# The last tile of a gated-recurrence and GEGLU kernel: its output in one piece or in two halves of the columns

## The chip, the cores and the metric

The kernel runs on one core of one Trainium2 chip. The metric is device time in microseconds (us) from launch to end, as a median over several runs. 0.3% of it is 0.78 us.

## What is computed

The first part is a complex gated recurrence over 768 steps for 4 batches and 8 heads of width 48. The second part takes its result, 3072 tokens of width 384, through a gated feed-forward block with a gated residual:

```python
S_re, S_im = a * S + k v^T                 # per step, a = a_re + i a_im, capped at 0.999
y[t] = q[t] @ S_re                         # -> x, 3072 x 384
ffn_out = gelu(x @ w_gate) * (x @ w_val) @ w_out      # d_ff = 1536
res_gate = 1 / (1 + exp(-(x @ w_res)))
out = x + res_gate * ffn_out               # float32
```

## The kernel before

The sequence is cut into chunks of 128 tokens, so there are 24 tiles of 128 tokens by 384 columns (4 batches, 6 chunks). The tiles are handled in units of one or two: units 0 and 1 are single first chunks, units 2 to 11 hold two tiles each, and the last pair is split into units 12 and 13 with one tile each. Three functions work on a unit `p`: `prepare` (loads, logarithms, running sums, features), `attend` (scores, state and x) and `forward` (the feed-forward block).

Nothing is run when these functions are called. Each call of `add` records a step: its engine, a kind, a function that issues the instructions, and the values that it reads and writes. `plan.run` then issues all 1450 steps in the order of a list, `ORDER`, written out by hand, and picks the buffers by it. The layer beneath derives the semaphore waits from the instructions in that order. `PLACE` moves some steps to another engine than their default, by step number. A second rule is in `run`: the kinds named in `PORT` (line 26; "otx", the sum with x, is one of them, while "ot", the gate product, is not) are chained, so that such a step on VectorE waits for the last such step on GpSimd, and the other way round.

The steps of `forward` that matter here, with the lines of the profile:

- L592: the products x @ w_gate and x @ w_val into PSUM banks ("gv"); L597: gelu on ScalarE; L598: its product with the value half on VectorE ("h").
- L607: x @ w_res ("res"); L609: the tanh that becomes the gate, `sg`, on ScalarE.
- L618: the output product, 12 matrix products of 384 columns into one PSUM bank, issued as three steps of four ("out").
- L622: the gate product on VectorE, (sg + 1) times the bank, into the SBUF tile `ot` ("ot").
- L625: the sum with x, in place in `ot` ("otx"), on GpSimd or, by `PLACE`, on VectorE. The last two tiles have it on VectorE.
- L627: the store of `ot`, 128 rows of 1536 bytes, from SyncE's queue ("store"). All 24 stores go out there; ScalarE issues no DMA in this kernel.

`ORDER` ends with unit 12. The tail of the list, in words: unit 13's output product, gate product and sum; unit 12's x @ w_res; unit 12's last four output products; its tanh; unit 13's store; unit 12's gate product, sum and store. At the end of the program (L665) SyncE waits for all DMA lanes and engines in a fixed row of waits, and all engines meet in barriers.

Of the kernel before, what the change touches and what calls it, by code (L numbers as in the profile page):

```python
# [15 lines left out]
OP = mybir.AluOpType  # L16
# [11 lines left out]


PLACE = {  # L30
    33: "DVE", 50: "DVE", 64: "ACT", 105: "DVE", 114: "DVE", 116: "POOL", 121: "DVE", 131: "DVE", 134: "ACT", 190: "DVE",
    191: "DVE", 213: "DVE", 221: "ACT", 223: "DVE", 225: "ACT", 230: "ACT", 245: "DVE", 305: "DVE", 306: "DVE", 323: "POOL",
    330: "DVE", 340: "DVE", 342: "ACT", 353: "DVE", 435: "ACT", 438: "ACT", 456: "DVE", 460: "DVE", 469: "DVE", 539: "DVE",
    551: "ACT", 554: "POOL", 555: "POOL", 562: "DVE", 570: "ACT", 572: "DVE", 576: "DVE", 599: "DVE", 654: "DVE", 667: "ACT",
    671: "POOL", 678: "DVE", 688: "DVE", 690: "ACT", 692: "DVE", 695: "ACT", 771: "DVE", 783: "ACT", 787: "POOL", 804: "DVE",
    806: "ACT", 811: "ACT", 817: "DVE", 831: "DVE", 872: "DVE", 899: "DVE", 902: "POOL", 903: "POOL", 943: "DVE", 1014: "POOL",
    1015: "POOL", 1022: "DVE", 1033: "ACT", 1041: "DVE", 1088: "DVE", 1124: "POOL", 1125: "POOL", 1143: "ACT", 1204: "DVE",
    1298: "DVE", 1314: "DVE", 1324: "ACT", 1325: "POOL", 1376: "DVE", 1386: "DVE", 1396: "ACT", 1397: "POOL", 1401: "DVE",
    1448: "DVE",
}  # L40
ORDER = [
    294, 293, 97, 16, 98, 303, 17, 102, 295, 21, 180, 103, 22, 104, 296, 304, 105, 23, 179, 106, 24, 107, 178, 25, 108, 109,
# [24 lines left out]
    1012, 902, 1208, 493, 503, 667, 385, 285, 592, 650, 379, 505, 903, 691, 591, 778, 96, 584, 1000, 381, 391, 692, 651, 687,  # L67
    1217, 473, 593, 907, 780, 404, 762, 393, 1013, 1311, 763, 487, 681, 585, 794, 596, 405, 890, 286, 781, 683, 594, 1312, 406,
    551, 777, 597, 1218, 600, 685, 595, 407, 908, 904, 688, 689, 905, 601, 398, 1110, 906, 408, 578, 686, 694, 399, 690, 764,
    782, 797, 698, 990, 507, 695, 579, 909, 291, 1378, 400, 699, 708, 706, 795, 1313, 766, 696, 709, 586, 618, 911, 509, 693,  # L70
    614, 292, 707, 796, 1014, 494, 489, 1105, 1122, 710, 587, 602, 697, 711, 589, 409, 512, 401, 880, 1123, 622, 1314, 799, 610,
    624, 878, 628, 620, 1001, 879, 495, 496, 891, 612, 606, 991, 513, 603, 1111, 910, 881, 623, 497, 629, 700, 616, 798, 615,
    608, 717, 599, 604, 801, 800, 895, 701, 712, 1219, 716, 514, 588, 805, 625, 1124, 515, 882, 802, 1125, 892, 897, 713, 803,
    896, 617, 1214, 619, 894, 605, 883, 783, 1220, 516, 1015, 804, 520, 893, 517, 806, 807, 621, 812, 521, 1383, 1379, 914, 808,
    1126, 598, 522, 1384, 1002, 814, 702, 523, 809, 822, 824, 815, 718, 524, 813, 912, 1019, 823, 734, 525, 518, 703, 626, 993,
    825, 1129, 607, 627, 916, 736, 738, 609, 1020, 920, 826, 720, 913, 726, 1130, 827, 918, 744, 1003, 1127, 816, 728, 611,
    1021, 740, 519, 915, 636, 1004, 1007, 613, 919, 705, 1016, 817, 1315, 1221, 1017, 630, 992, 1006, 704, 637, 1008, 833, 1018,
    1009, 1385, 631, 1005, 1128, 638, 1131, 832, 1010, 1022, 719, 936, 898, 1386, 727, 1024, 1222, 917, 934, 639, 921, 1230,
    937, 632, 1132, 1382, 402, 721, 723, 1215, 633, 1023, 735, 1231, 935, 1210, 1322, 846, 634, 737, 1394, 924, 1211, 1133, 729,
    739, 1011, 715, 925, 842, 1134, 1101, 741, 926, 640, 818, 730, 927, 995, 1323, 722, 819, 899, 714, 742, 1395, 1212, 724,  # L80
    1112, 850, 745, 725, 928, 403, 852, 1223, 828, 938, 848, 752, 1100, 1026, 929, 732, 834, 1113, 743, 641, 731, 836, 1025,
    838, 939, 944, 847, 1028, 840, 858, 844, 945, 733, 835, 859, 829, 746, 837, 1030, 810, 860, 1027, 811, 1117, 1032, 1114,
    849, 1227, 1232, 1115, 753, 1118, 1233, 1031, 1119, 1224, 1229, 747, 820, 1228, 1316, 1309, 839, 1387, 831, 1029, 1116, 748,
    841, 1226, 922, 1225, 1234, 1135, 1324, 994, 940, 855, 1235, 1388, 1103, 1396, 854, 923, 830, 749, 1045, 1325, 754, 635,
    941, 966, 856, 755, 1397, 1104, 861, 930, 1236, 1047, 1237, 857, 1120, 950, 1213, 1238, 1048, 750, 968, 1038, 1036, 1046,
    946, 1033, 751, 1137, 843, 1308, 948, 1039, 1049, 821, 851, 1102, 1239, 1050, 952, 1037, 958, 1139, 1240, 845, 868, 1317,
    960, 1398, 853, 1055, 1040, 931, 1326, 942, 951, 1041, 1241, 869, 1244, 1054, 1399, 1042, 1034, 962, 1318, 1136, 862, 964,
    870, 943, 1327, 953, 863, 1121, 1035, 1138, 959, 1051, 1328, 1319, 1242, 1142, 756, 871, 864, 1043, 1251, 1060, 865, 1380,
    1068, 1400, 1141, 1320, 961, 970, 1321, 1056, 872, 1140, 1246, 972, 1064, 1243, 1058, 1381, 1057, 971, 1401, 973, 873, 1076,
    1389, 1066, 1044, 1072, 1143, 1245, 954, 1329, 1052, 1249, 1074, 1080, 1059, 956, 947, 1333, 1062, 1146, 1250, 932, 1155,  # L90
    1081, 963, 1147, 1078, 1144, 1390, 1157, 757, 967, 1145, 1158, 1247, 1148, 949, 1391, 955, 965, 1392, 1310, 1393, 1065,
    1149, 1061, 1248, 957, 969, 980, 1403, 1332, 1150, 1330, 1063, 1077, 1402, 1156, 1073, 1331, 1079, 981, 1151, 1404, 1164,
    1159, 1334, 974, 1406, 1070, 1258, 1075, 982, 866, 1160, 1067, 1260, 1165, 1152, 933, 1082, 1261, 975, 983, 1336, 1252,
    1083, 976, 1253, 1084, 1053, 867, 1161, 1259, 984, 1069, 977, 1186, 1071, 1182, 1188, 1153, 1262, 1335, 1184, 1085, 1337,
    1338, 1263, 1170, 978, 1192, 1265, 1405, 1254, 1183, 1407, 1090, 1255, 1408, 1175, 1185, 1086, 1154, 1409, 1091, 1087, 1256,
    1088, 1171, 1257, 1162, 1089, 1166, 1264, 1174, 1168, 1187, 979, 1176, 1092, 985, 1172, 1189, 1193, 1178, 1177, 1167, 1093,
    1180, 1173, 1190, 1094, 1413, 1191, 1266, 1271, 1411, 1270, 1341, 1272, 1274, 1342, 1179, 1276, 1169, 1292, 1268, 1273,
    1287, 1414, 1275, 1163, 1278, 1410, 1277, 1267, 1181, 1286, 1412, 1194, 1269, 1288, 1415, 1280, 1289, 1195, 1293, 1416,
    1200, 1417, 1339, 1279, 1340, 1283, 1282, 1196, 1284, 1290, 1285, 1343, 1281, 1201, 1344, 1197, 1294, 1345, 1291, 1198,
    1300, 1438, 1199, 1295, 1095, 1430, 1301, 1431, 1302, 1202, 1303, 1296, 1304, 1203, 1358, 1362, 1419, 1364, 1204, 1350,  # L100
    1440, 1297, 1205, 1354, 1360, 1298, 1427, 1432, 1418, 1356, 1299, 1422, 1420, 1305, 1434, 1421, 1435, 1436, 1351, 1352,
    1423, 1424, 1353, 1355, 1433, 1426, 1359, 1428, 1346, 1429, 1347, 1348, 1425, 1439, 1361, 1363, 1441, 1367, 1349, 1444,
    1437, 1357, 1442, 1365, 1366, 1445, 1368, 1443, 1369, 1372, 1446, 1373, 1447, 1370, 1448, 1374, 1371, 1449, 1375, 1376,
    1377,
]


# [19 lines left out]
class Plan:  # L127
# [10 lines left out]
    def add(self, eng, kind, fn, reads=(), writes=(), size=1, act=None):  # L138
        deps = set()
        for v in reads:  # L140
            deps.update(v.writers)
        for v in writes:
            deps.update(v.writers)
            deps.update(v.readers)
        stores = [v.store for v in list(reads) + list(writes) if v.store is not None]
        stores = sorted(set(stores), key=stores.index)
        t = Step(eng, kind, fn, deps, stores, size, act)
        t.index = len(self.steps)
        for v in writes:
            v.writers, v.readers = [t], []  # L150
        for v in reads:
            if t not in v.writers:
                v.readers.append(t)
        for x in stores:
            x.users.append(t)
        self.steps.append(t)
        return t
# [30 lines left out]
def kernel(  # L188
# [13 lines left out]
    nc = tc.nc  # L202
# [3 lines left out]
    DM = H * D  # L206
    FF = moe_w_gate.shape[1]
    KF = DM // 128
    NF = FF // 128
# [6 lines left out]
    NU = len(units)  # L216
    where = {bc: (p, i) for p, u in enumerate(units) for i, bc in enumerate(u)}
    size = [len(u) for u in units]

    ctx.enter_context(tc.manual_schedule())  # L220
    cst = ctx.enter_context(tc.tile_pool(name="cst", bufs=1))
# [26 lines left out]
    wo = cst.tile([128, NF, DM], BF, name="wo")  # L248
# [76 lines left out]
    on = {"DVE": nc.vector, "POOL": nc.gpsimd, "ACT": nc.scalar}  # L325
    add = plan.add

    def place(default):

        return PLACE.get(len(plan.steps), default)  # L330
# [6 lines left out]
    W = {}  # L337
# [226 lines left out]
    def forward(p):  # L564
        s, n = st[p], size[p]
        s["xT"], s["h2"] = Buf("xT"), Buf("h2")
        xT = [s["xT"].part() for _ in range(n)]
        for i in range(n):
            if p >= PE_X:
                add("SP", "dX", lambda i=i: nc.sync.dma_start(  # L570
                    out=s["xT"].tile[:, :, i, :], in_=s["x"].tile[:, i].rearrange("p h d -> p (h d)"), transpose=True), [s["xi"][i]], [xT[i]])
# [3 lines left out]
            def f(i=i, xp=xp):  # L575
                xp.make([128, KF, 128], BF)
                for k_ in range(KF):
                    nc.tensor.transpose(out=xp.tile[:, k_, :],
                                        in_=s["x"].tile[:, i].rearrange("p h d -> p (h d)")[:, k_ * 128:(k_ + 1) * 128], identity=ident)
# [3 lines left out]
        h2 = []  # L583
        for m in range(NF // 2):
            gp, vp, hh = Bank(), Bank(), s["h2"].part()
            h2.append(hh)
            for name, w_, o_ in (("wg", wg, gp), ("wv", wv, vp)):
# [11 lines left out]
                out=hv(), in0=hv(), scalar=0.5, in1=vp.tile, op0=OP.mult, op1=OP.mult), [vp], [hh], n)  # L599
        sg = [Buf("sg") for _ in range(n)]  # L600
# [9 lines left out]
                [rp], [sg[i]], 1, "G")  # L610
        for i, (b, c) in enumerate(units[p]):
            op_, ot = Bank(), Buf("ot")
            for lo in range(0, NF, 4):
                def f(i=i, lo=lo, op_=op_):
                    if lo == 0:
                        op_.make([128, DM])
                    for k_ in range(lo, lo + 4):
                        nc.tensor.matmul(out=op_.tile, lhsT=s["h2"].tile[:, k_, i * 128:(i + 1) * 128], rhs=wo[:, k_, :],  # L618
                                         start=(k_ == 0), stop=(k_ == NF - 1))
                add("PE", "out", f, [h2[lo // 2], h2[lo // 2 + 1], W["wo", lo]], [op_])  # L620
            ti = b * NC + c
            add("DVE", "ot", lambda i=i, op_=op_, ot=ot: nc.vector.scalar_tensor_tensor(  # L622
                out=ot.tile, in0=sg[i].tile, scalar=1.0, in1=op_.tile, op0=OP.add, op1=OP.mult), [sg[i], op_], [ot])
            e8 = place("POOL")
            add(e8, "otx", lambda i=i, ot=ot, e8=e8: on[e8].tensor_tensor(  # L625
                out=ot.tile, in0=ot.tile, in1=s["x"].tile[:, i].rearrange("p h d -> p (h d)"), op=OP.add), [s["xi"][i]], [ot])
            add("SP", "store", lambda ot=ot, ti=ti: nc.sync.dma_start(out=out[ti * 128:(ti + 1) * 128, :], in_=ot.tile), [ot], [])  # L627

    weights()
    for p in range(NU):  # L630
# [39 lines left out]
```

## Time and profile before

| what | value |
|---|---|
| median of 3 runs (lowest to highest) | 260.29 us (260.19 to 260.85) |
| the profiled execution | 261.98 us, of which the span 260.2 us |
| mean granted TensorE clock | 0.974, lower in slices 6 to 8 of 40 and full after them |
| busy share of the span: TensorE, VectorE, ScalarE, GpSimd | 85%, 87%, 81%, 35% |
| store, issue to landing, 24 of them: min / median / max | 1.9 / 2.5 / 4.3 us |
| last matrix product ends, last sum ends, last store issued | 255.8, 257.1, 257.1 us |

How to read it: times of instructions are counted from the start of the span. The 1.8 us between the span and the execution's time lie outside what the profile shows. The engine rows say how long an engine was busy, not that it set the end; what sets the end is read from the chain of work that ended last and from the timeline of the last microseconds. "SPq" is SyncE's queue of DMA issues and waits.

### The profile page before, as it was taken

The numbers are of one execution on the slowest core, as the hardware profiler recorded it, in microseconds if no ns is written. First come the engines' busy times: TensorE is split into PE (matmuls) and PEld (weight loads), VectorE is DVE, ScalarE is ACT, GpSimd is POOL, SyncE is SP. The second block draws the span as 40 slices with busy tenths as digits, with TensorE's granted clock in tenths as the row PEclk, the third lists the DMA queues.
The fourth block names the chain that finished last, engine by engine and source line by source line (L and its number), as shares of the span: only waits on it lengthen the run. The fifth ranks groups of instructions, "written<-read, shape, count | busy, mean of one in ns | idle before, by whom it ended". The sixth has DMA issues, their size and how long they took to land.

```text
span 260.2 us, 6343 instructions
## 1 busy us (share of the span) xinstructions
PE 222.3 (85%) x2415; PEld 174.7 (67%) x2415; DVE 225.7 (87%) x401; ACT 211.3 (81%) x354; POOL 90.4 (35%) x116
## 2 busy tenths in 40 slices
PE   0233842877999999999999999999999999999993
PEld 0011532757878877887887778768778778877881
DVE  2789999997999999999999999999999976573463
ACT  4899999998999999999999999797999932532330
POOL 1022266594611662486626177006020230101100
PEclk9999975799999999999999999999999999999999
DMA  8999999999999998999986779779789539201311
GB/s 140 188 186 186 188 185 167 205 181 217 152 183 185 164 199 161 192 178 183 214 147 121 153 155 168 181 145 232 131 134 222 97 88 170 75 3 35 113 40 60
DMA packets 162174, 39.83 MB, mean 153 GB/s; under 512 B 155616, under 2 KB 162144, under 8 KB 162144
## 3 DMA queue, kind: packets, MB, share of 16 engines
q1 hardware_dynamic: 157696, 35.53, 78.1%
q0 software_dynamic: 4448, 3.90, 9.7%
q8 instruction: 19, 0.31, 0.6%
q14 instruction: 11, 0.09, 0.1%
HBM read 31.26 MB, written 4.72 MB: 138 GB/s over the span
## 4 chain that ended last, share of the span: by engine, by line
PE 60%; DVE 19%; DMA 7%; SPq 5%; issue 4%; POOL 1%; ACT 0%; DVEq 0%; POOLq 0%; ACTq 0%
PE pb L592 30%; PE pb L618 16%; SPq L374 5%; PE pb L607 3%; PE pb L360 3%; PE pb L522 3%; DMA t<-fr 2%; PE pb L492 2%; DVE h L598 2%; DMA k<-in_k_dram 2%; DMA ai<-in_a_im_dram 2%; DVE fQ L475 2%; DVE Qe L470 2%; DVE ll L408 1%; DMA vf<-in_v_dram 1%
## 5 line engine op out<-in xcount | busy, mean ns | idle before, releaser
L597 ACT ACTIVATE h<-pb 128x512 bf16<-128x512 f32 (+1 forms) x84 | 41.1, 550 | 23.5 <-PE pb L592 23.1
L592 PE MATMUL pb<-xT,wg 128*128 128x256 bf16 (+1 forms) x504 | 56.0, 257 | 1.2 <-DVE U L552 0.9
L592 PE MATMUL pb<-xT,wv 128*128 128x256 bf16 (+1 forms) x504 | 57.0, 257 | 0.0
L618 PE MATMUL pb<-wo,h 128*128 128x384 bf16 x288 | 55.5, 326 | 0.0
L598 DVE SCALAR_TENSOR_TENSOR h<-h,pb 128x512 bf16<-128x512 bf16 (+1 forms) x84 | 48.0, 601 | 7.3 <-ACT h L597 4.6
L592 PEld LDWEIGHTS <-wg 128*128 128x128 bf16 x504 | 43.1, 98 | 8.1 <-issue 1.6
L592 PEld LDWEIGHTS <-wv 128*128 128x128 bf16 x504 | 42.2, 98 | 6.1
L639 ACT ACT_TABLE_LOAD x34 | 43.6, 1283 | 1.3 <-PEq L654 0.7
L525 DVE TENSOR_TENSOR am<-pb,mask 128x512 bf16<-128x512 f32 x48 | 31.6, 680 | 4.5 <-PE pb L522 4.3
L618 PEld LDWEIGHTS <-h 128*128 128x128 bf16 x288 | 26.0, 97 | 13.8 <-issue 0.3
L625 POOL TENSOR_TENSOR ot<-ot,x 128x384 f32<-128x384 f32 x18 | 16.9, 941 | 46.1 <-issue 19.9
L444 POOL TENSOR_TENSOR tl<-t,th 128x768 fp32r<-128x768 f32 (+1 forms) x9 | 13.2, 1479 | 22.7 <-DVE Gb L554 14.3
L522 PE MATMUL pb<-QT,KT 96*128 96x128 bf16 x192 | 16.7, 219 | 2.7 <-DVE KT L335 2.4
L622 DVE SCALAR_TENSOR_TENSOR ot<-sg,pb 128x384 f32<-128x384 f32 x24 | 13.1, 547 | 6.3 <-PE pb L618 6.2
L360 PE MATMUL pb<-lh,ut_hf 128*128 128x384 f16 x24 | 8.6, 360 | 11.1 <-DVE lh L406 11.1
L398 POOL TENSOR_TENSOR t<-t,ai 128x768 f32<-128x768 f32 (+1 forms) x9 | 14.7, 1637 | 8.8 <-DMA ai<-in_a_im_dram 3.5
L522 PEld LDWEIGHTS <-KT 96*128 96x128 bf16 x192 | 12.7, 97 | 6.5 <-DVE KT L335 2.9
L492 PE MATMUL pb<-ident,fK 128*128 128x128 bf16 x112 | 10.7, 252 | 6.8 <-DVE fK L475 6.0
L609 ACT ACTIVATE sg<-pb 128x384 f32<-128x384 f32 x24 | 11.9, 499 | 5.2 <-PE pb L607 3.2
L607 PE MATMUL pb<-wr,xT 128*128 128x384 bf16 x72 | 15.6, 326 | 0.3 <-DVE am L525 0.2
L334 ACT CAST x<-pb 128x384 bf16<-128x384 f32 x19 | 9.2, 482 | 6.4 <-PE pb L536 6.1
L360 PE MATMUL pb<-th,ut_hf 128*128 128x384 f16 x24 | 8.6, 359 | 6.4 <-DVE th L335 6.0
(89 smaller groups left out, 467.3 us busy)
## 6 DMA issues: line engine op xcount, KB each, us to landing
ar<-in_a_re_dram SPq DMA_DIRECT2D x24, 192.0 KB, 4.6
ai<-in_a_im_dram SPq DMA_DIRECT2D x24, 192.0 KB, 4.7
q<-in_q_dram SPq DMA_DIRECT2D x24, 192.0 KB, 4.6
k<-in_k_dram SPq DMA_DIRECT2D x24, 192.0 KB, 4.1
vf<-in_v_dram SPq DMA_DIRECT2D x24, 192.0 KB, 4.0
out_dram<-ot SPq DMA_DIRECT2D x24, 192.0 KB, 2.5
wg<-in_moe_w_gate_dram POOLq DMA_DIRECT2D x6, 192.0 KB, 7.1
wv<-in_moe_w_val_dram POOLq DMA_DIRECT2D x6, 192.0 KB, 6.2
```

The source lines that it names most:

```text
L360: nc.tensor.matmul(out=bank.tile, lhsT=ones, rhs=x[:, i * DM:(i + 1) * DM], start=(j == 0), stop=(j == 1))
L398: add(e1, "tai", lambda: on[e1].tensor_tensor(out=F("t"), in0=F("t"), in1=flat(T("ai"), n), op=OP.mult), [s["ai"]], [s["t"]], n)
L492: nc.tensor.transpose(out=tp.tile[:, h, :], in_=s[g].tile[:, i * H + h], identity=ident)
L522: nc.tensor.matmul(out=ap.tile[:, h, :], lhsT=kT.tile[0:DD, u * H // 2 + h, :], rhs=qT.tile[0:DD, u * H // 2 + h, :], start=True, stop=True)
L525: add("DVE", "am", lambda u=u, am=am, ap=ap: nc.vector.tensor_tensor(out=am.tile[:, u * H // 2:(u + 1) * H // 2, :], in0=ap.tile, in1=mask ...
L592: nc.tensor.matmul(out=o_.tile[:, u, :], lhsT=w_[:, k_, (2 * m + u) * 128:(2 * m + u + 1) * 128], rhs=s["xT"].tile[:, k_, 0:n].rearrange(" ...
L597: add("ACT", "gelu", lambda gp=gp, hv=hv: nc.scalar.activation(out=hv(), in_=gp.tile, func=AF.Gelu), [gp], [hh], n, "G")
L598: add("DVE", "h", lambda vp=vp, hv=hv: nc.vector.scalar_tensor_tensor(out=hv(), in0=hv(), scalar=0.5, in1=vp.tile, op0=OP.mult, op1=OP.mul ...
L607: nc.tensor.matmul(out=rp.tile, lhsT=s["xT"].tile[:, k_, i, :], rhs=wr[:, k_, :], start=(k_ == 0), stop=(k_ == KF - 1))
L618: nc.tensor.matmul(out=op_.tile, lhsT=s["h2"].tile[:, k_, i * 128:(i + 1) * 128], rhs=wo[:, k_, :], start=(k_ == 0), stop=(k_ == NF - 1))
L625: add(e8, "otx", lambda i=i, ot=ot, e8=e8: on[e8].tensor_tensor(out=ot.tile, in0=ot.tile, in1=s["x"].tile[:, i].rearrange("p h d -> p (h d ...
L639: plan.run(ORDER, lambda table: nc.scalar.preload_act_table_set(ACT_SETS[table]), after)
```

## The change

For unit 12 alone, whose tile is the last to be stored, the last step of four output products becomes two steps: the same four products for columns 0 to 191, and then for columns 192 to 383, into the same PSUM bank. The gate product becomes two instructions of 192 columns, both on VectorE. The sum with x becomes two: columns 0 to 191 on GpSimd, the others on VectorE; their kind is "oth", which `PORT` does not name. The store becomes two of 128 rows of 768 bytes: the first half from SyncE's queue, the second from ScalarE's. The unit's other two steps of four products are as before. The remaining edits of the diff are step numbers in `PLACE` and `ORDER`, shifted by four; the order of all other instructions on every engine is the same.

```diff
+    TAIL = 12
...
             op_, ot = Bank(), Buf("ot")
+            cols = [slice(0, DM)] if p != TAIL else [slice(0, DM // 2), slice(DM // 2, DM)]
+            acc, res = [op_], [ot]
             for lo in range(0, NF, 4):
...
+                if lo == NF - 4 and len(cols) > 1:
+                    acc, res = [Val(op_.store) for _ in cols], [Val(ot.store) for _ in cols]
+                    for x in acc:
+                        x.writers = list(op_.writers)
+                for x, sl in zip(acc, cols if len(acc) > 1 else [slice(0, DM)]):
+                    def f(i=i, lo=lo, op_=op_, sl=sl):
...
+                            nc.tensor.matmul(out=op_.tile[:, sl], lhsT=s["h2"].tile[:, k_, i * 128:(i + 1) * 128], rhs=wo[:, k_, sl],
+                                             start=(k_ == 0), stop=(k_ == NF - 1 and sl.stop == DM))
+                    add("PE", "out" if len(acc) == 1 else "outh", f, [h2[lo // 2], h2[lo // 2 + 1], W["wo", lo]], [x])
...
+            for j, (x, y, sl) in enumerate(zip(acc, res, cols)):
+                add("DVE", "ot", lambda i=i, op_=op_, ot=ot, sl=sl: nc.vector.scalar_tensor_tensor(
+                    out=ot.tile[:, sl], in0=sg[i].tile[:, sl], scalar=1.0, in1=op_.tile[:, sl], op0=OP.add, op1=OP.mult), [sg[i], x], [y])
+            for j, (x, y, sl) in enumerate(zip(acc, res, cols)):
+                e8 = place("POOL" if j == 0 else "DVE")
+                add(e8, "otx" if len(cols) == 1 else "oth", lambda i=i, ot=ot, e8=e8, sl=sl: on[e8].tensor_tensor(
+                    out=ot.tile[:, sl], in0=ot.tile[:, sl], in1=s["x"].tile[:, i].rearrange("p h d -> p (h d)")[:, sl], op=OP.add), [s["xi"][i]], [y])
+            for j, (x, y, sl) in enumerate(zip(acc, res, cols)):
+                e = "SP" if j == 0 else "ACT"
+                add(e, "store", lambda ot=ot, ti=ti, sl=sl, e=e: (nc.sync if e == "SP" else nc.scalar).dma_start(
+                    out=out[ti * 128:(ti + 1) * 128, sl], in_=ot.tile[:, sl]), [y], [])
```

In the new `ORDER` the tail reads: both halves of the products, the tanh, unit 13's store, both gate products, both sums, both stores.

## The prediction

> **What bounds the kernel now.** The order of all instructions but the last few is the same in both programs, so I read the end of the span. First the chain of work that ended last, for its last two microseconds (start, length, what):
>
> ```profile
> 255.18 0.66 PE pb L618 x4
> 255.84 0.04 DVEq L622
> 255.88 0.04 issue
> 255.93 0.56 DVE ot L622
> 256.49 0.02 issue
> 256.51 0.56 DVE ot L625
> ```
>
> The last four output products hand over to the gate product, and that to the sum with x, with no gap worth having. Then the timeline of the same stretch, for who else is there:
>
> ```profile
> 255.02 0.81 PE L618 MATMUL pb<-wo,h 128*128 128x384 bf16 x4
> 255.22 0.49 ACT L609 ACTIVATE sg<-pb 128x384 f32<-128x384 f32 x1 [2.32 <-PE pb L607]
> 255.31 2.12 SPq L627 DMA_DIRECT2D out_dram<-ot  x2
> 255.93 0.55 DVE L622 SCALAR_TENSOR_TENSOR ot<-sg,pb 128x384 f32<-128x384 f32 x1 [0.64 <-PE pb L618]
> 256.51 0.56 DVE L625 TENSOR_TENSOR ot<-ot,x 128x384 f32<-128x384 f32 x1
> ```
>
> The gate is ready at 255.71, before the products end at 255.83; GpSimd is idle, ScalarE free from 255.71. Last the DMA view from 255.0 on (slices of 0.13 us), the store's rows, and SyncE's waits:
>
> ```profile
> DMA  0000000018998100000000299970000000000000
> DMA to landing us min/median/max: 1.9/1.9/1.9
> SPq L665 <- DMA out_dram<-ot: 1.0, 1, 1.0
> L665 SPq EVENT_SEMAPHORE  x12: 17/28/28, 257.5 to 260.1; - x12
> ```
>
> Two humps, unit 13's store and unit 12's. In the trace's records the last store is issued at 257.098 (0.333 long), its first packet starts at 257.931 (0.833 after issue), its last ends at 258.607 (a spread of 0.676), and SyncE's wait for it ends at 258.974 (0.367 later). The waits at the end are a row of ten, from 257.476 on, about 0.062 apart; nine are done while the store is under way, and the tenth, whose lane is the last store's, is the one that waits. Barriers take the span to 260.2. So 3.14 us lie between the last product and the end of the waits, and only they can change.
>
> **The change, part by part.** All times are of the profiled execution, 261.98 us (span 260.2); the median of the runs shown, 260.29, is 1.69 below, and I carry the difference over to it.
>
> *Products, 0.* Products of 384, 256 and 128 columns follow each other at 0.1625, 0.109 and 0.056 us: in proportion to columns. Eight of 192 take 8 x 0.081 = 0.65, as four of 384 do. Above, 0.109 each would add 0.22; the proportion excludes it, and the 128-column row shows that the doubled weight loads (97 ns each) hide.
>
> *Overlap of the halves, 0.* In the built program the first gate product waits until TensorE's count is 2419, the value after all eight products; the second carries no wait on TensorE. So VectorE starts at 255.93 as before. Had it started after the first four, 0.33 would be gained.
>
> The Trainium skill (PSUM — Partial Sum Buffer, "PSUM bank collisions raise a hardware error") says that two engines may not touch one bank at once; that speaks against any such overlap in one bank. No run here shows it, and the sum has 0 either way.
>
> *Gate product, -0.20 for the first half.* The width rows:
>
> ```profile
> L598 DVE SCALAR_TENSOR_TENSOR h<-h,pb 128x512 bf16<-128x512 bf16 x60 | 39.5, 678 | 4.6 <-PE pb L592 2.3 <-ACT h L597 1.9 <-issue 0.4
> L598 DVE SCALAR_TENSOR_TENSOR h<-h,pb 128x256 bf16<-128x256 bf16 x24 | 8.5, 410 | 2.7 <-ACT h L597 2.7
> L625 POOL TENSOR_TENSOR ot<-ot,x 128x384 f32<-128x384 f32 x18 | 16.9, 941 | 46.1 <-issue 19.9 <-DVE ot L622 16.9 <-DVE fK L475 6.6
> ```
>
> 268 ns for 256 columns is 1.05 ns each, so 192 fewer take 0.20 off the 0.553: 0.35. Independent VectorE instructions overlap by 0.08 (the 410 ns rows start 331 ns apart). First half 255.93 to 256.28, second 256.20 to 256.55.
>
> *Sum, first half on GpSimd.* It starts 0.13 after VectorE ends (243.21 to 243.34; at least 0.03, VectorE's own hand-over): 256.38 to 256.41, I take 256.38 with a wait already queued. The sum takes 0.912 in the median; GpSimd's `tl` rows are 1642 ns at 768 columns and 908 at 384, 1.91 ns a column, so 0.912 - 0.37 = 0.545 (bounds 0.249, its 48-column copy, and 0.912). It ends at 256.93; SyncE issues 0.03 later, at 256.95, 0.15 before the old issue.
>
> *Sum, second half on VectorE, the unknown.* It is ready at 256.55 + 0.03 = 256.58 and takes 0.557 - 0.20 = 0.36. GpSimd is then at work, and both add two SBUF operands. The trace has 66 GpSimd compute rows; many run beside VectorE rows with one operand in PSUM, which keep their usual length, none beside a VectorE row with two in SBUF, since `PORT` chains those kinds. "oth" is outside `PORT`. Bounds: run freely, 256.58 to 256.94 and ScalarE's issue at 256.97; or held to GpSimd's end, 256.93 to 257.29, issue at 257.32. I take the held one: the nearest pair, unit 11's sums, has GpSimd ending at 244.26 and VectorE starting at 244.29. That is a chain in the code, so it proves no lock, and I keep both ends.
>
> The Trainium skill (SBUF — State Buffer, "Who interferes with whom") states that a VectorE instruction with two SBUF inputs contends with a GpSimd one that reads SBUF, and that whichever came first keeps the pair to its end. By it the second sum starts at 256.93, as I chose; without it, at 256.58.
>
> *Stores.* A full store's 0.676 is 8 packets an engine at 62 ns and 0.18 of skew. Packets of 256 bytes take 18 ns and of 1536 bytes 62, so 768 bytes take about 36: a half alone spreads over 0.18 + 8 x 0.036 = 0.47 (bounds 0.32 and 0.676), two at once over 0.18 + 16 x 0.036 = 0.76. ScalarE has issued no DMA; I price its issue like SyncE's idle one (0.833 to the first packet); SyncE's very first, at 0.742, took 1.114, so up to 0.28 more. Held: 257.32 + 0.833 + 0.47 + 0.367 = 258.99.
>
> The Trainium skill (DMA: Bandwidth & Descriptors, "Issuing engines are not separate DMA queues") says that a second issuing engine saves only issue time, as all queues run on the same 16 engines. By it the second queue is worth at most the issue row's 0.333; here the halves are 0.37 apart when held, so nothing.
>
> *The row of waits, +0.43.* ScalarE's store is on lane 0, SyncE's half on lane 7. Lane 0 is the third of the ten waits. Before, only the last one waited; now SyncE stands at the third until ScalarE's half has landed, and walks seven more: 7 x 0.062 = 0.43. The bounds are 0 (if the rest passed at once) and this.
>
> *Sum:* 258.99 + 0.43 = 259.42 against 258.974: **+0.45**. Profiled execution 262.43, median 260.29 + 0.45 = **260.74 us**, +0.17%: no change that a measurement of this kernel can tell (0.3%, 0.78 us).
>
> **Rivals.**
>
> 1. *The second sum is not held.* Issue at 256.97, both halves on the engines at once: landing at 256.97 + 0.833 + (0.47 to 0.76) + 0.367 = 258.64 to 258.93, with the waits 259.07 to 259.36: +0.10 to +0.39, 260.53 in the middle. For: no row shows a hold. Against: the kernel keeps such pairs apart everywhere else.
> 2. *Slower: ScalarE's queue is cold.* Its first DMA is this one, at the end, with nothing behind it to hide the delay. At SyncE's first row 0.28 more: +0.73, 261.02. The longest issue-to-packet time of a store is 2.064 (on a busy queue), 1.23 more: 261.97. From 0.33 beyond the forecast it is slower by over 0.3%. Against: the stores issued on an idle queue all show 0.833 to 0.859.
> 3. *Not held, and the waits cost nothing.* 258.64 to 258.93: -0.33 to -0.04, 260.11. It needs the row of waits to pass at less than its 0.062.
> 4. *The change does what it says*, and the first gate product starts at 255.60. Everything is 0.33 earlier than in rival 1: -0.23 to +0.06, 260.2. The wait on 2419 speaks against it.
>
> **How the numbers follow.** Forecast 0.50, rival 1 0.23, rival 2 0.15, rival 3 0.07, rival 4 0.05. The range takes in rival 1, 3's middle less a little, and the warm end of rival 2: 260.15 to 261.10. Slower by over 0.3% needs 261.07: most of the upper part of rival 2 and a tail of the forecast, as runs of one kernel spread by 0.66: 0.13. Faster needs 259.51, which no case reaches; 0.03 for what I did not see. Same: 0.84.
>
> **What would show it.** In the profile after: the first gate product at 255.9, not 255.6; the second sum starting at GpSimd's end (held) or at 256.6; ScalarE's issue at 257.3; two half humps in the DMA view; seven waits on SyncE after the one that waits. A first packet of ScalarE's store over 1.1 after its issue makes rival 2. A difference elsewhere in the span would make all of it wrong.

## The result and the profile after

| | before | after |
|---|---|---|
| median (lowest to highest), 7 runs each | 260.87 us (260.19 to 261.22) | 261.93 us (261.66 to 262.48) |
| profiled execution, and its span | 261.98, 260.2 us | 262.28, 260.5 us |
| mean granted TensorE clock | 0.974 | 0.970 |
| tail: end of the last matrix product to end of the span | 4.376 us | 5.453 us |

The ratio is 1.0048 [1.0031, 1.0065]: the change costs 1.25 us (0.81 to 1.70). It is slower, by more than the 0.3% that would count as no change, and the time lies above the predicted range.

The two spans differ by 0.3 us only, since in the profiled execution of before the last product ended at 255.831 and in that of after at 255.044. That part varies from one execution to the next. But for the halving of the last products, whose cost e4 below measures, the change touches only what comes later, so I compare tails: **5.453 - 4.376 = 1.08 us**, inside the interval of the ratio. From here on a time "at 0.53" is counted from the end of the last matrix product of its own execution.

The chain of work that ended last, of after (start, length, what):

```profile
254.38 0.67 PE pb L625 x8
255.06 0.04 DVEq L630
255.09 0.04 issue
255.14 0.63 DVE ot L630 x2
255.77 0.02 issue
255.79 0.54 DVE ot L634
```

The chain has the form that it had before, with a pair of gate products of 0.63 us in place of one of 0.56, and a last sum of 0.54, hardly shorter than the whole sum's 0.56. The timeline of the same stretch:

```profile
255.14 0.62 DVE L630 SCALAR_TENSOR_TENSOR ot<-sg,pb 128x192 f32<-128x192 f32 x2 [0.65 <-PE pb L625]
255.57 0.55 POOL L634 TENSOR_TENSOR ot<-ot,x 128x192 f32<-128x192 f32 x1 [12.11 <-DVE ot L630]
255.79 0.54 DVE L634 TENSOR_TENSOR ot<-ot,x 128x192 f32<-128x192 f32 x1
256.36 0.37 ACTq L638 DMA_DIRECT2D out_dram<-ot  x1
```

GpSimd has had nothing to do for 12.11 us and then takes its half, beside VectorE's. All this ends at 256.33, or 1.287, where the old sum ended at 1.239: so far 0.05 us are lost. The DMA view of after from 254.2 on (slices of 0.16 us) and its issues:

```profile
DMA  0000000599600000019996000000000000000000
...
out_dram<-ot SPq DMA_DIRECT2D x1, 96.0 KB, 1.6
out_dram<-ot ACTq DMA_DIRECT2D x1, 96.0 KB, 1.7
```

The two half stores overlap and make one hump, which is over at 257.72. From there to the end of the span none of the kernel's data move, and yet 2.8 us pass. What is there is seen in the rows of the program's end (duration in ns min/median/max, first and last start), of before, here behind the row of GpSimd's last sum in the timeline:

```profile
243.34 0.91 POOL L625 TENSOR_TENSOR ot<-ot,x 128x384 f32<-128x384 f32 x1 [3.62 <-issue]
...
L665 POOLq DRAIN  x3: 46/106/4212, 243.3 to 259.6; - x3
L665 SPq DRAIN  x3: 7/7/13, 259.0 to 259.4; - x3
```

And of after:

```profile
L677 SPq EVENT_SEMAPHORE  x12: 17/28/28, 256.5 to 260.4; - x12
L677 POOLq EVENT_SEMAPHORE  x4: 17/17/17, 259.4 to 260.4; - x4
L677 POOLq DRAIN  x3: 46/106/3856, 255.5 to 260.2; - x3
L677 SPq DRAIN  x3: 7/7/13, 258.6 to 259.6; - x3
```

Every engine ends the program with a drain, a step that ends only after the engine's own last instruction, and then meets the others. In before the drains of TensorE, VectorE and ScalarE are over 0.03 to 0.06 us after the last instruction of their engine. GpSimd's longest drain row is the one to read, against the end of its last sum (before: 244.257). Before, it begins at 243.3, with GpSimd's last sum, and lasts 4.212 us: to 247.53, which is **3.274 us after that sum had ended**. Nobody waits for it there. After, it begins at 255.5 and lasts 3.856 us, to 259.39: again 3.274 us after GpSimd's last sum ended. Meanwhile SyncE has done with its waits, at 258.66 (3.612), and stands until GpSimd comes to the meeting, at 259.43.

A wait counts as passed where its row starts.

| counted from the last product's end, us | before | after |
|---|---|---|
| first gate product starts | 0.095 | 0.093 |
| last sum on VectorE ends; sum on GpSimd ends | 1.239; none | 1.287; 1.072 |
| the wait for the store that lands last is passed | 3.143 | 3.045 |
| the last of SyncE's waits is passed | 3.143 | 3.472 |
| SyncE's drains done | 3.283 | 3.612 |
| GpSimd's drain done | -8.300 | 4.346 |
| GpSimd's first step of the meeting | 3.308 | 4.390 |
| end of the span | 4.376 | 5.453 |

SyncE is 0.33 later, and GpSimd 0.75 later than SyncE would need (4.390 - 3.612 - the old 0.025): together 1.08. The later of the two sets the end: without the 0.33 the drain would still end at 4.346.

### The profile page after: what moved, and what is told of

The parts are those of the page before. It is cut to its first block, busy times and chain, and to the rows that moved or that the text cites. A ratio compares the mean times of both kernels' runs of the same rounds, so it can differ in the third digit from the quotient of the medians.

```text
span 260.5 us, 6356 instructions
## 1 busy us (share of the span) xinstructions
PE 222.2 (85%) x2419; PEld 175.2 (67%) x2419; DVE 225.3 (86%) x402; ACT 211.4 (81%) x354; POOL 90.8 (35%) x117
## 4 chain that ended last, share of the span: by engine, by line
PE 68%; DVE 16%; DMA 6%; SPq 5%; issue 3%; POOL 1%; ACT 0%; DVEq 0%
PE pb L592 34%; PE pb L625 17%; SPq L374 5%; PE pb L607 4%; PE pb L360 3%; PE pb L522 3%; DMA t<-fr 2%; PE pb L492 2%; DMA k<-in_k_dram 2%; DMA ai<-in_a_im_dram 2%; DVE h L598 2%; DVE Qe L470 1%; DVE fQ L475 1%; PE pb L536 1%; PE pb L534 1%
## 5 line engine op out<-in xcount | busy, mean ns | idle before, releaser
L625 PE MATMUL pb<-wo,h 128*128 128x384 bf16 (+1 forms) x292 | 55.5, 324 | 0.0
L634 POOL TENSOR_TENSOR ot<-ot,x 128x384 f32<-128x384 f32 (+1 forms) x19 | 17.4, 919 | 57.9 <-DVE ot L630 29.0
L630 DVE SCALAR_TENSOR_TENSOR ot<-sg,pb 128x384 f32<-128x384 f32 (+1 forms) x25 | 13.1, 528 | 6.1 <-PE pb L625 6.0
```

Source lines behind the costliest of these rows:

```text
L625: nc.tensor.matmul(out=op_.tile[:, sl], lhsT=s["h2"].tile[:, k_, i * 128:(i + 1) * 128], rhs=wo[:, k_, sl], start=(k_ == 0), stop=(k_ == N ...
L634: add(e8, "otx" if len(cols) == 1 else "oth", lambda i=i, ot=ot, e8=e8, sl=sl: on[e8].tensor_tensor(out=ot.tile[:, sl], in0=ot.tile[:, sl] ...
```

## The experiments

The theory from these rows, G: GpSimd's drain ends 3.27 us after its last instruction of work, however long that is, and the end of the program waits for it. Its rivals: Q, the new queue or the second store is the cost; H, it is the hold of VectorE's sum. Beside them there is W, the row of waits: SyncE stands at the wait for the later half store and then walks the seven waits behind it. Each store reports its landing on a lane, a counter that one wait of the row stands for. All ratios are against runs of before on the same chip, and each experiment's profile is its own.

**Both sums on VectorE (e1).** After, with the first half's sum moved to VectorE:

```diff
-                e8 = place("POOL" if j == 0 else "DVE")
+                e8 = place("POOL" if len(cols) == 1 else "DVE")
```

> The changed kernel with the first half's sum with x on VectorE too, so that GpSimd does nothing in the last 12 us. I measure the tail from the end of the last matrix product to the end of the span: before 4.38 us, changed kernel 5.46. Theory G (GpSimd's drain at the end of the program, 3.27 us after its last compute, sets the end of the changed kernel): the drain is over before the stores land, SyncE's row of waits sets the end again, and the tail is 0.10 + four VectorE instructions at a pitch of 0.27 and 0.08 more, 1.17, + 0.03 + 0.90 + 0.46 + 0.37 for ScalarE's store + 0.43 for seven waits + 1.23 to the end = 4.7 us, ratio about 1.001. Rival Q (ScalarE's queue costs it, by its first use or at the end): the tail stays at 5.3 or more, ratio 1.004. Rival H (the hold of the second sum by GpSimd is what costs): the tail falls by 0.2 only, to 5.3.

Ratio 1.0017 [1.0005, 1.0030], tail 4.599. Its timeline:

```profile
254.61 0.62 DVE L630 SCALAR_TENSOR_TENSOR ot<-sg,pb 128x192 f32<-128x192 f32 x2 [0.65 <-PE pb L625]
255.15 0.62 DVE L634 TENSOR_TENSOR ot<-ot,x 128x192 f32<-128x192 f32 x2
255.80 0.38 ACTq L638 DMA_DIRECT2D out_dram<-ot  x1
```

GpSimd's drains, from the rows of its program's end:

```profile
L677 POOLq DRAIN  x3: 46/102/4211, 242.0 to 258.5; - x3
```

The long drain is back at 242.0, and 0.85 us of the tail are gone, though both stores, the second queue and the row of waits are still there. Alone, the two sums take 353 and 352 ns; beside GpSimd the second took 540. What is left of the loss, 0.22 us of tail, is the row of waits: the third is passed at 2.977 and the last at 3.403, where before had 3.143.

**The whole sum on GpSimd (e2).** Before, with only the engine of the last sum changed:

```diff
-    ... 1325: "POOL", 1376: "DVE", ...
+    ... 1325: "POOL", 1376: "POOL", ...
```

> The kernel before with one thing changed: the last tile's whole sum with x is on GpSimd; no halves, one store from SyncE. Theory G: the sum ends 0.10 + 0.55 + 0.13 + 0.91 = 1.69 us after the last product, the drain 3.27 later, and 1.11 from there to the end as in the changed kernel: a tail of 6.07 us against 4.38, ratio 1.0065. Rivals Q and H see only the longer sum and GpSimd's later start: 0.45 more, a tail of 4.83, ratio 1.0017.

Ratio 1.0061 [1.0048, 1.0074], tail 6.021. From its timeline:

```profile
255.20 0.91 POOL L625 TENSOR_TENSOR ot<-ot,x 128x384 f32<-128x384 f32 x1 [12.30 <-DVE ot L622]
256.14 0.33 SPq L627 DMA_DIRECT2D out_dram<-ot  x1
```

From the rows of its program's end:

```profile
L665 POOLq DRAIN  x3: 46/106/4221, 255.2 to 260.2; - x3
```

No halves, no second queue, one store, and no sum on VectorE that could be held. The sum ends at 1.639, 0.400 later than VectorE's, which delays the last of SyncE's waits to 3.527; the drain ends at 4.914, 3.275 after the sum, and the tail grows by 1.65. By SyncE alone it would have grown by 0.38.

**Both half stores from SyncE (e3).**

```diff
-                e = "SP" if j == 0 else "ACT"
+                e = "SP"
```

> The changed kernel with both half stores from SyncE's queue, so that ScalarE issues no DMA. Theory G: nothing changes, as GpSimd's drain ends last whatever the stores do: a tail of 5.46 us, ratio 1.004 to 1.005 as in the changed kernel. Rival Q: the tail falls to about 4.7 to 4.8, ratio 1.001.

Ratio 1.0037 [1.0025, 1.0049], tail 5.430: as after's 5.453. From the rows of its end:

```profile
L677 POOLq DRAIN  x3: 46/102/3859, 255.0 to 259.6; - x3
```

ScalarE's queue is not the cost. The second store is issued at 1.528 instead of 1.319, and SyncE's drains are done 0.17 later than in after, but GpSimd's sum ends at 1.076 as it did, and its drain at 4.350: the tail does not see SyncE's part. VectorE's sum still takes 542 ns.

**A tiny instruction on GpSimd (e5).** Before, with one copy of 128x1 on GpSimd behind the last sum; nothing reads it:

```diff
+    self_ot, tiny = [], cst.tile([128, 1], FP, name="tiny")
...
+    add("POOL", "tiny", lambda: nc.gpsimd.tensor_copy(out=tiny, in_=self_ot[0].tile[:, 0:1]), [self_ot[0]], [])
```

> The kernel before with one instruction added: GpSimd copies one column (128 x 1) of the last tile into an unused tile, after the last sum; nothing that is computed waits for it. Theory G, with a drain that is the same after any last compute: the copy ends about 1.24 + 0.13 + 0.15 = 1.5 us after the last product, the drain 3.27 later, 1.11 to the end: a tail of 5.9 us, 1.5 more than before, ratio 1.006. If the drain grows with the size of the last instruction, or belongs to two-input sums alone, the tail stays within 0.3 us of the 4.38 of before. Rivals Q and H expect no change.

From its timeline:

```profile
254.11 0.19 POOL L637 COPY tiny<-ot 128x1 f32<-128x1 f32 x1 [12.88 <-DVE ot L625]
```

From the rows of its program's end:

```profile
L669 POOLq DRAIN  x3: 102/194/3482, 254.1 to 258.4; - x3
```

The copy ends at 1.492, the drain at 4.765, 3.273 later, and the tail is 6.000, 1.62 longer than before's. So an instruction of 188 ns, off every path of data, costs about as much tail as a sum of 910 ns. (It brings GpSimd to the meeting at 4.810, 1.50 later than in before; the other 0.12 passes inside the meeting, for which see the end of the next section.) The ratio is 0.9996 [0.9986, 1.0006] all the same: everything ahead of the tail was faster, and the last product ended at 252.807, 3.0 us ahead of before's profile. I had not expected that; the runs with `pad` below find where it comes from.

**The products alone in halves (e4).** After, with the gate product, the sum and the store of unit 12 made whole again:

```diff
+            if len(cols) > 1:
+                op_.writers = [q_ for x in acc for q_ in x.writers]
+                cols, acc, res = [slice(0, DM)], [op_], [ot]
             for j, (x, y, sl) in enumerate(zip(acc, res, cols)):
```

> The kernel before with only the products of the change: the last four in two halves of the columns, into one bank; gate product, sum and store whole, as before. My step says 0: the gate product starts 0.10 us after the last product, the tail from the last product to the end is 4.38 us, and the eight products take as long as four, 0.65 us. If the doubled weight loads cost something, the eight take 0.8 us or more.

260.53 us, one run, beside a median of 260.76 for before; tail 4.374, gate product at 0.094. The split of the products costs nothing that this run shows.

**The two store steps swapped in `ORDER` (e8),** on top of both sums on VectorE:

```diff
-    1377, 1378, 1379, 1380, 1381,
+    1377, 1378, 1379, 1381, 1380,
```

> As e1 (both sums on VectorE), with ScalarE's store recorded before SyncE's, so that it gets lane 7, the last of the row of waits, and SyncE's earlier half gets lane 0. Theory W (seven waits walked behind the store that lands last cost 0.43): SyncE's half lands 1.01 + 0.83 + 0.41 + 0.37 = 2.62 us after the last product, the row is walked to 3.05, ScalarE's half has landed at 2.98 by then: the last row at 3.1 instead of 3.40, tail 4.3 instead of 4.60, level with the kernel before (4.38), ratio 1.000. If the waits cost nothing, the tail stays at 4.6.

Ratio 1.0007 [0.9995, 1.0019], tail 4.632. This didn't make the test that it was meant for: in the built program ScalarE's store is on lane 0 and SyncE's on lane 7 as before, since the layer beneath gives the lanes. The third wait is passed at 2.972 and the last at 3.399, so it is a repeat of both sums on VectorE; the two tails, 4.599 and 4.632, show how closely a tail repeats. (One of its twelve runs took 586 us and is not in the ratio.) That the late store on the last lane would save the 0.43 is left untried.

**A bank for each half (e7).** On top of that, unit 12's two halves of columns get a PSUM bank each, and all 12 products go in halves:

```diff
+                if lo == 0 and len(cols) > 1:
+                    acc, res = [op_, Bank()], [Val(ot.store) for _ in cols]
...
-                            nc.tensor.matmul(out=op_.tile[:, sl], ...
+                                nc.tensor.matmul(out=x.tile, ...
```

> As e8, and the last tile's two halves of columns have a PSUM bank each, so that the first gate product can start when the first half's products are done. If the one bank is what took the overlap away, the first gate product starts when the gate is there, about 0.10 us before the last product's end instead of 0.09 after it, the stores are issued 0.19 earlier than in e8, and the tail is 4.1 us, ratio 0.999. If the second half's products are in the way, or nothing but the order counts, it starts at 0.09 as in e8 and the tail is 4.3.

Ratio 1.0001 [0.9990, 1.0013], tail 4.400; the expectation counted on the swapped lanes, which it didn't get. Its timeline:

```profile
254.33 0.62 DVE L629 SCALAR_TENSOR_TENSOR ot<-sg,pb 128x192 f32<-128x192 f32 x2 [0.47 <-ACT sg L609]
254.87 0.62 DVE L633 TENSOR_TENSOR ot<-ot,x 128x192 f32<-128x192 f32 x2
255.52 0.37 ACTq L637 DMA_DIRECT2D out_dram<-ot  x1
```

The last product ends at 254.433, and the first gate product starts at 254.33, 0.101 ahead of it: here is the overlap that the halves of one bank do not give in this program. The releaser in brackets is now ScalarE's tanh (`sg`) and no longer TensorE, so the tanh is next late. Both sums end at 1.054 instead of 1.249: 0.195 gained. The row of waits, still there, gives it back: before's tail is 4.376.

**Where the tiles lie (e9, e11).** The tile `tiny` above had moved all work tiles by 32 bytes, from an address that is 32 past a multiple of 64 to a multiple of 64. To have that alone, before gets an unused tile of 128x1, cleared once; and, as the counter-check, two of them, which move the work tiles by 64 bytes:

```diff
     wr = cst.tile([128, KF, DM], BF, name="wr")
+    pad0 = cst.tile([128, 1], FP, name="pad0")
+    nc.gpsimd.memset(pad0, 0.0)
```

> The kernel before with an unused tile of 128 x 1 after the weights, cleared once at the start, so that all work tiles lie 32 bytes further on, at multiples of 64, as they did in e5; its tail is as before. In e5 the tail grew by 1.62 us and the time did not, since the last product ended 3.0 us earlier. Theory A (the place of the tiles did that): the loads' 192-byte packets take 15 ns nearly all, the first gate product comes near 75.4 us instead of 77, and the time falls by 1.6 us, ratio 0.994. If e5's late GpSimd instruction or chance did it, ratio 1.000.

> The kernel before with two unused tiles instead of one, so that all work tiles lie 64 bytes further on and again 32 past a multiple of 64. If what counts is the place modulo 64 bytes, everything is as before: packets of 192 bytes at 28 ns in the slowest tenth, first gate product near 77 us, ratio 1.000. If any shift or an added clearing instruction does it, ratio 0.994 as in e9.

One tile: ratio 0.9942 [0.9926, 0.9959], tail 4.482. Two: ratio 1.0000 [0.9988, 1.0012], tail 4.326. The DMA view of before over the first 60 us (packets, MB, share of 16 engines; issues with median us to landing):

```profile
q1 hardware_dynamic: 46712, 8.84, 100.4%
...
ar<-in_a_re_dram SPq DMA_DIRECT2D x16, 192.0 KB, 4.6
```

The same view of the kernel with one tile of padding:

```profile
q1 hardware_dynamic: 49911, 9.44, 81.0%
...
ar<-in_a_re_dram SPq DMA_DIRECT2D x16, 192.0 KB, 3.8
```

Most load packets are of 192 bytes. Over the whole span their median is 15 ns in both kernels, but one in ten takes 28 ns or more before, and 15 with one tile. In the first 60 us 7% more packets are through in less engine time, and the first gate product of all starts at 75.2 us where before it was 77.7. With two tiles it is 77.0 and 29 ns. So, as far as these three positions go, the gain hangs on the address modulo 64 bytes, and it belongs to no part of the change. That it comes by way of the faster packets is read from these rows and not tested apart; why they are faster no run shows.

**Put together (e10, e13).** Two banks, both sums on VectorE, one tile of padding; once with the two half stores, once with one whole store from SyncE. The second differs from the first by:

```diff
-            for j, (x, y, sl) in enumerate(zip(acc, res, cols)):
-                e = "SP" if j == 0 else "ACT"
...
+            add("SP", "store", lambda ot=ot, ti=ti: nc.sync.dma_start(out=out[ti * 128:(ti + 1) * 128, :], in_=ot.tile), res, [])
```

> e7 (two banks, four instructions on VectorE, half stores from SyncE and ScalarE, ScalarE's on lane 0) with the work tiles of e9. Theory W: the row of waits costs 0.43 behind ScalarE's store, so the tail is e7's 4.40 or up to 0.1 more, about 0.1 to 0.2 longer than with one whole store in e13; ratio 0.994 from the place of the tiles. If half stores are a gain in themselves, the tail is shorter than e13's.

> e9 (work tiles at multiples of 64 bytes) with the last tile's halves in two banks and all four gate products and sums on VectorE, but one whole store from SyncE, on lane 7 as before. Theory G and W: nothing late on GpSimd, no row of waits behind the store; the sums end 1.05 us after the last product as in e7 instead of 1.24, the last wait ends at 2.96 instead of 3.14, the tail is 0.18 shorter than e9's 4.48; ratio 0.9935. If the waits cost nothing, it would be no better than e10.

With two stores: 259.39 us, ratio 0.9935 [0.9922, 0.9948], tail 4.569. With one: **258.96 us, ratio 0.9918 [0.9905, 0.9932]**, tail 4.299, the fastest of all. The timeline of the latter:

```profile
252.81 0.62 DVE L632 SCALAR_TENSOR_TENSOR ot<-sg,pb 128x192 f32<-128x192 f32 x2 [0.47 <-ACT sg L612]
253.35 0.62 DVE L636 TENSOR_TENSOR ot<-ot,x 128x192 f32<-128x192 f32 x2
```

The sums end at 1.055 and 1.057. The two half stores have landed, and the wait that stands for them is passed, at 2.779; the whole store's at 2.953, 0.17 later. But behind the former come seven more waits, to 3.206, and behind the latter none. So the halves win 0.17 and lose 0.43. Most of the gain of the fastest kernel is the padding's; the rest is not separated from it by the ratios, whose intervals overlap, and is 4.482 - 4.299 = 0.18 us in the tails.

## Why the prediction was wrong

- **The step that failed: "Barriers take the span to 260.2", with "GpSimd is idle".** I took what follows SyncE's waits as fixed, and priced the sum on GpSimd to the point where it hands over to SyncE's store. What that instruction sets going at the end of its own engine's program was not priced: the drain, which ends 3.274 us after it. Runs: 0.85 of tail gone when GpSimd is let off, +1.65 and +1.62 when it alone is given work, and a drain that ends 3.273 to 3.276 after the last instruction in all thirteen kernels, for instructions of 188 to 917 ns. The row was in the profile before: 4212 ns for a drain that begins with the last sum, 12 us from the end, is not the length of a barrier. Read against the sum's end (244.257) it says 3.27, and then the new sum's forecast end, 256.93, gives 260.20 for the drain and the old 1.09 from SyncE's last drain to the end: 261.29 for the span, +1.08.
- **Products, 0:** right (tail 4.374 with them alone).
- **Overlap of the halves, 0:** right; the first gate product starts 0.093 after the last product. With a bank each it starts 0.101 before. The 0.33 that the prediction puts on such an overlap, and rival 4's start at 255.60, are wrong by its own line: the gate is ready only at 255.71. The runs with two banks gained 0.195. The Trainium skill (PSUM — Partial Sum Buffer, "PSUM bank collisions raise a hardware error") forbids two engines in one bank at once; the runs agree as far as the program's own wait goes, which the second bank removes. What the chip does without that wait was not tried.
- **Gate product:** 353 and 347 ns, started 272 ns apart; forecast 0.35 and 0.27.
- **Sum on GpSimd:** 546 ns, forecast 545; SyncE's issue at 1.098, forecast 1.12.
- **Second sum held to GpSimd's end:** right in kind, mis-sized. It took 540 ns in place of 352, and ended 0.215 after GpSimd. But it started on time, at 0.747; I had it start where GpSimd ends and run its full 0.36 from there. Price 0.19, forecast 0.35. The Trainium skill (SBUF — State Buffer, "Who interferes with whom") has the second engine blocked until the first is done; the trace agrees in that VectorE ends after GpSimd, but only part of its instruction lies behind the hold. The 0.215 is about the 0.20 that the prediction's width rows give for 192 columns, as if the columns had waited for GpSimd's end and the fixed part had not. Nothing but these durations speaks for a lock.
- **Stores:** half-store packets of 36.1 and 37.6 ns in the mean and a spread of 0.46; forecast 36 and 0.47. ScalarE's first packet came 0.896 after its issue: 0.06 of rival 2's up to 0.28 or 1.23. The loss happens to be of rival 2's size, and isn't its mechanism. The Trainium skill (DMA: Bandwidth & Descriptors, "Issuing engines are not separate DMA queues") gives a second issuer no more than the time of an issue; the runs agree: with both half stores from SyncE (e3) its drains are done 0.17 later than in after, and an issue takes 0.333.
- **The row of waits, +0.43:** right, 0.427 measured in after, 0.426 and 0.427 in two others. SyncE's part came to +0.33 (forecast +0.45: the hold 0.17 cheaper, the queue 0.06 dearer).
- **Rivals 1, 3 and 4** did not come about: the sum was held, the waits had their price, the halves did not overlap. Of the points under "What would show it", the first gate product, the seven waits and ScalarE's first packet came as named. Three did not: the second sum started at 0.747, or 256.58 in before's times, the sign named for a free sum, and was held all the same; ScalarE's issue came at 1.319, or 257.15, and not at 257.3; the half stores show one hump and not two. No point looked at GpSimd behind its sum.

Of the tail's 1.08 the cause is settled: GpSimd's drain. Two things stay open. What fills the drain's 3.27 us no run shows, nor whether it is the same in a kernel that uses GpSimd otherwise. And the meeting itself, from GpSimd's first step in it to the end of the span, takes 1.03 to 1.07 us in nine kernels and 1.19 to 1.20 in the four whose work tiles lie at multiples of 64 bytes (e5, e9, e10, e13), for no reason that the runs show.

## What to carry to other kernels

When a step moves to an engine near the end of a program, price that engine's own ending as well: look up its longest drain row, take the time from the end of its last work to the end of that row, and see whether last work plus that lag still ends before the final wait of the others. Here GpSimd's last instruction has to end 3.3 us ahead of that point. Before splitting the last store, look where the wait for the later half stands in the row: here the halves were through 0.17 us earlier and the seven waits behind took 0.43; that they pay with that wait last was not tried. And compare tails from a common event, when the spans of single executions differ by more than the change.

## What had not been expected of the hardware

- GpSimd's drain ends 3.27 us after its last instruction, be that a copy of one column or a sum of 384.
- Work tiles moved by 32 bytes, to a multiple of 64: 192-byte load packets' 90th percentile 28 to 15 ns, the load queue's share of the whole span 78.1% to 68.4%, and 0.58% of the time; moved by 64 bytes: 29 ns, and no change in time.
